# A fused attention and expert kernel: the first item's first 256 rows turned by VectorE, cast by GpSimd

## The chip, the core and the metric

The kernel runs on one core of a Trainium2 chip. The metric is the device time of one execution in microseconds, the median of several runs; lower is better.

## The reference

Two stages. The first is an attention with random features; its output, as rows of 512, goes into a mixture of experts with a capacity.

```python
# 4 batches, 8 heads, 576 positions, 64 columns; omega is 128 x 64
def phi(x):                       # x already scaled by 64 ** -0.25
    h = x @ omega.T - sum(x * x) / 2
    return exp(h - max(h)) / sqrt(128)
kv  = phi(k).T @ v                # per batch and head: 128 x 64
z   = sum(phi(k), over positions)
out = (phi(q) @ kv) / (phi(q) @ z + 1e-6)

# x: 2304 rows of 512, out of the heads; 8 experts, w1 512 x 1024, w2 1024 x 512, capacity 576
logits = x @ w_gate;  e = argmax(logits);  p = softmax(logits)[e]
# each expert takes its rows in order, up to the capacity
y   = relu(x @ w1[e]) @ w2[e]
out = p * y for the rows kept, 0 for the others
```

## The kernel before

Only TensorE can multiply matrices; it writes PSUM, eight banks of 2 KB a partition. Everything is f32, and the expert products are made from split operands: a rounded part (`hi`) and the rest (`lo`), so that one product is three matmuls (hi by hi, lo weights by hi, hi weights by lo).

**Keys.** A first loop (steps below 0) projects the keys, takes their maxima and exponentials and sums `kv` for each batch and head. The gate's weights are multiplied into `kv` as extra columns, so that the routing scores come out of the same numerators as the attention.

**Queries.** Then come 18 query tiles of 128 rows, one a step. The code's step `t` runs from 0 to 20, and the work on one tile is spread over four steps:

- In step t TensorE projects tile t (`project`, output pjq, two banks) from a chunk of queries (`qraw`, three tiles a chunk; `load_q(c + 2)` is issued in the last step of chunk c). ScalarE copies one half to `d`, VectorE takes the maxima of both halves (L192), GpSimd adds the maxima to one half of `d` (L837), ScalarE adds those of the other half (L852).
- In step t + 2 TensorE transposes `d` (L782, output qtr, two banks) and ScalarE takes the exponentials (L843, qpT).
- In step t + 3 TensorE multiplies by `kv` (`numer`, L654, output qacc) and VectorE normalises (`normalise`: denominators L678, reciprocal L679, product `xr` L682, scores L685). SP stores the rows to `x_d` in DRAM. The rows that are stored in step s are thus those of tile s - 3. The numerators of steps 3 to 17 and 19 share one PSUM tile (`pair`, one buffer), those of steps 18 and 20 have banks of their own.

All engines run their instructions in program order. Smaller jobs are generators that the loop resumes at fixed places (`run`): a job that yields "E" goes on at the end of a step, one that yields "P" behind the GpSimd addition, at most `most` such pieces in a step.

**The first item.** The rows are given out to experts later, but the first item's expert is known as soon as row 0 is scored, since the kernel's first item is batch 0 with the expert of its first row (rows of it that go to another expert get a scale of 0, and rows that no such item holds go through a branch at the end). `first_item` reads that expert and loads its four `w1` chunks (`load_w`, 512 KB each) at steps given by `W1_LOADS`. `first_splits` splits each chunk on GpSimd in five pieces: one `hi` of 128x1024 (L135) and four `lo` of 128x256 (L140), 20 pieces in all. Before the change it begins with the load of the second chunk, so that its pieces come from step 9 on.

The item needs its rows transposed (features on the partitions), as `xhi` and `xlo`, 576 columns. Its columns are made in two ways before the change:

- Rows 0 to 255 (two tiles): in steps 3 and 4 GpSimd copies `xr` into a scratch tile `xt` (L690); in steps 6 to 9 (`FIRST_AT`) TensorE transposes 64 rows a step, four instructions of 64x64 among those of `d` (L782, output xtri), and `copy_x` makes `xhi` on ScalarE (L430) and `xlo` on VectorE (L432).
- Rows 256 to 575: `first_rows` loads them from `x_d` behind step 15 with SP (`load_x`, four DMAs, 32 partitions each, L401). In steps 18 and 19 VectorE turns them in 32x32 blocks (`turn_x`, L406, 640 columns each time, into `xt`), ScalarE makes `xhi` (L411) and GpSimd `xlo` (L412).

Behind the numerators of step 20 TensorE starts the first item's products (`mm1`, L705 to L707), first those with columns 0 to 255 of `xhi` and `xlo`. The other items follow, each with its rows loaded and turned by the second way.

Of the kernel before, what the change touches and what calls it, by code (L numbers as in the profile page):

```python
# [22 lines left out]
NT = N // 128  # L23
# [13 lines left out]
AHEAD = [(0, 0)]  # L37
NJ = 11
FIRST_LOAD = 15
W1_LOADS = (0, 6, 9, 12)  # L40
W2_LOADS = 16
FIRST_AT = (6, 7, 8, 9)
BRANCH_AT = 4
EPS = 1e-6 * M
BIG = 1048576.0
# [18 lines left out]
def attention_moe(ctx, tc, kT, qT, va, om, wg, w1, w2, cap, ident, tri, desc, lst, tab0, out):  # L64
# [83 lines left out]
    def start(gen):  # L148
        tasks.append([gen, None])
# [245 lines left out]
                in_offset=bass.IndirectOffsetOnAxis(ap=big["idx"][0:n, i, 2:3], axis=0),  # L395
            )

    def load_x(rows, b0=0):
        src = x_d[rows, :].rearrange("(b r) (q c) -> q r b c", r=32, q=4)
        for q in range(4):  # L400
            nc.sync.dma_start(big["xz"][32 * q : 32 * q + 32, b0:, :], src[q])  # L401


    def turn_x(b0, b1, o=0, eng=nc.vector):
        t = big["xt"][:, o : o + b1 - b0, :].rearrange("p b (k r) -> p b k r", k=4)
        nc.vector.transpose(t, big["xz"][:, b0:b1, :].rearrange("p b (a k) -> p b k a", k=4))  # L406
        t = t.rearrange("p b k r -> p k b r")
        hi, lo = (big[x][:, :, 32 * b0 : 32 * b1].rearrange("p k (b r) -> p k b r", r=32) for x in ("xhi", "xlo"))

        def split():  # L410
            nc.scalar.copy(hi, t)  # L411
            eng.tensor_tensor(lo, t, hi.bitcast(F32), op=ALU.subtract)  # L412

        return split

    def transpose_x(i, nm, at):
        n = sub_n[i]
# [186 lines left out]
    def first_item():  # L604
        yield from pause(6)
        e0 = const.tile([1, E + 2], F32, name="e0")
        e0i = const.tile([1, 1], I32, name="e0i")
        lg0 = lg[0:1, 0, :]
        nc.vector.tensor_reduce(e0[:, E : E + 1], lg0, op=ALU.max, axis=AX.X)
        yield  # L610
        nc.vector.scalar_tensor_tensor(
            e0[:, 0:E], lg0, e0[:, E : E + 1], desc_sb[0:1, :], op0=ALU.is_ge, op1=ALU.mult
        )
        yield
        nc.vector.tensor_reduce(e0[:, E + 1 : E + 2], e0[:, 0:E], op=ALU.max, axis=AX.X)
        yield
        nc.vector.tensor_scalar(e0i, e0[:, E + 1 : E + 2], -1.0, float(E), op0=ALU.mult, op1=ALU.add)
        yield
        ev = nc.sync.value_load(e0i[0:1, 0:1], min_val=0, max_val=E - 1)
        for c in range(4):  # L620
            while step[0] < W1_LOADS[c]:
                yield "E"
            load_w(1, c, ev)
            if c == 1:
                start(first_splits())
            yield "E"
        while step[0] < W2_LOADS:
            yield "E"
        for c in range(4):
            load_w(2, c, ev)  # L630
            yield "E"
# [9 lines left out]
                split_w_lo(1, c, nc.gpsimd, k)  # L641

    xr_l = {}

    def first_rows():
        load_x(slice(32 * NBA, SLOTS), NBA)
# [15 lines left out]
    def normalise(t, acc, whole):  # L664
# [19 lines left out]
            )  # L684
        nc.vector.tensor_reduce(lg[:, t, :], xr[:, D + 1 : ROW, :], op=ALU.add, axis=AX.X)  # L685
        nc.sync.dma_start(x_d[t * 128 : (t + 1) * 128, :], xr[:, 0:D, :].rearrange("p c h -> p (c h)"))
        if t < 2:

            xr_l[t] = big["xt"][:, 4 * t : 4 * t + 4, :]
            nc.gpsimd.tensor_copy(xr_l[t], xr[:, 0:D, :].rearrange("p c h -> p (c h)").rearrange("p (m k) -> p k m", k=4))  # L690

    HALVES = [(0, 256), (256, SLOTS)]

# [42 lines left out]
    for n in range(NK + NT + 3):  # L736
# [24 lines left out]
        if 0 <= t - 2 < NT:  # L761
            d = d_l.pop(t - 2)
            trs = [bank((3 + i, (2, SM)[i])[t > NT], f"qtr{n}{i}") for i in range(2)]

            parts = [
                [(trs[i][:, u * 64 : (u + 1) * 64], d[64 * i : 64 * i + 64, u, :], i) for u in range(H)] for i in range(2)
            ]

            if t in FIRST_AT:
                k0 = FIRST_AT.index(t)  # L770
                i = k0 % 2
                tr = bank(SM, f"xtri0{k0}")
                rows = slice(64 * i, 64 * i + 64)
                x0 = xr_l[k0 // 2]
                parts[i][0:0] = [
                    (tr[:, k * 64 : (k + 1) * 64], x0[rows, k, :], i) for k in range(4)
                ]
                start(copy_x(tr, 64 * k0, 64))
            for x in chain(*zip_longest(*parts)):
                if x is not None:  # L780
                    rows = slice(64 * x[2], 64 * x[2] + 64)
                    nc.tensor.transpose(x[0], x[1], id_sb[rows, rows])  # L782
# [47 lines left out]
        else:  # L830
            if t < NT:
# [4 lines left out]
                maxima(mx, 0, d[:, 0:4, :])  # L836
                nc.gpsimd.tensor_tensor(d[:, 0:4, :], d[:, 0:4, :], spread(mx, 0), op=ALU.add)  # L837
                d_l[t] = d
            run("P", times=2, most=2)
            if 0 <= t - 2 < NT:  # L840
                qpT = qp.tile([128, 2, H * 64], F32, tag="qpT", name=f"qpT{t}", bufs=2)
                for i in range(2):
# [15 lines left out]
            if 0 <= t - 3 < NT:  # L858
                normalise(t - 3, acc_l[0], whole)
                if t == 3:  # L860
                    start(first_item())
            if t in (NT, NT + 1):

                b0 = NBA + 5 * (t - NT)
                split_x = turn_x(b0, b0 + 5, b0 - NBA, nc.gpsimd)
# [8 lines left out]
        if n < NK:  # L874

            for k in range(KB, 2 * B):
                if (9 * (k - KB) + 8) // KG + 2 == n:
                    load_k(k // 2, k % 2)
            if n == 3:
                start(setup())  # L880
            if n in (NK - 4, NK - 2):
                load_q(0 if n == NK - 4 else 1)
        if t == FIRST_LOAD:
            first_rows()
    qstack.close()
# [317 lines left out]
```

## Time and profile before

| | us |
|---|---|
| median of 3 runs | 261.82 (260.41 to 262.20) |
| the profiled execution | 260.95 |
| its span, first to last instruction | 259.2 |
| TensorE busy, matmuls | 253.7 |
| TensorE busy, weight loads (beside the matmuls) | 232.7 |
| VectorE busy | 167.2 |
| ScalarE busy | 148.8 |
| GpSimd busy | 42.6 |

The key loop ends and the query steps begin at about 46 us; step 6 begins at 62.0, step 10 at 74.3, step 17 at 93.6, and the first item's products at 101.5. TensorE's granted clock is the full 2.4 GHz in all slices. A row of the profile gives the start of an instruction or of a run of equal ones, how long it took, its engine, its line and what it writes and reads; PE is TensorE, DVE VectorE, ACT ScalarE, POOL GpSimd, and SPq the queue of SyncE, which issues most of the DMAs.

### The profile page before, as it was taken

To read this page: it belongs to the slowest core of one execution; us is meant where nothing else is said; L and a number is where in the kernel's file an instruction comes from. 1 tells how busy PE (TensorE), PEld (TensorE's weight loads), DVE (VectorE), ACT (ScalarE), POOL (GpSimd) and SP (SyncE) were. 2 spreads that over 40 slices of the span, in tenths; PEclk is the share of its full clock that TensorE was granted. 3 is DMA by queue.
4 is the path that set the end of the run, shared out by engine and by line. 5 is a ranking of instruction groups with operands and counts; after the bars stand their busy time and mean duration, and the time that the engine had idled before them with its cause. 6 is when DMAs were issued, how large, how long until landed. Compare 5 with 4: busy or idle time off the path is not lost. (4 is left out here: it accounts for less than half of the span.)

```text
span 259.2 us, 7581 instructions
## 1 busy us (share of the span) xinstructions
PE 253.7 (98%) x3058; PEld 232.7 (90%) x3058; DVE 167.2 (65%) x351; ACT 148.8 (57%) x374; POOL 42.6 (16%) x61
## 2 busy tenths in 40 slices
PE   7999999999999999999999999999999999999994
PEld 6999999999999999999988789999888999998882
DVE  3999888779999998655763745566850064667500
ACT  3788888899999995326402536552361155524611
POOL 1002000255369896200000000000000000000000
PEclk9999999999999999999999999999999999999999
DMA  7999870034976769990059619992012897950121
GB/s 204 390 382 349 285 254 3 5 122 149 311 234 207 275 169 289 373 390 21 1 134 276 206 49 311 213 286 66 3 40 66 293 245 206 326 164 0 49 93 48
DMA packets 35171, 48.54 MB, mean 187 GB/s; under 512 B 2290, under 2 KB 23410, under 8 KB 35122
## 3 DMA queue, kind: packets, MB, share of 16 engines
q1 hardware_dynamic: 34002, 46.39, 57.0%
q10 hardware_dynamic: 1120, 1.52, 1.9%
q8 instruction: 28, 0.46, 0.7%
q14 instruction: 21, 0.17, 0.2%
HBM read 35.97 MB, written 11.93 MB: 185 GB/s over the span
## 5 line engine op out<-in xcount | busy, mean ns | idle before, releaser
L705 PE MATMUL hi<-xhi,w1hi 128*128 128x256 f32 (+1 forms) x192 | 56.7, 295 | 0.0
L706 PE MATMUL hi<-xhi,w1lo 128*128 128x256 f32 (+1 forms) x192 | 56.4, 294 | 0.0
L707 PE MATMUL hi<-xlo,w1hi 128*128 128x256 f32 (+1 forms) x192 | 56.3, 293 | 0.0
L718 DVE SCALAR_TENSOR_TENSOR hlo<-hi,hhi 128x256 fp32r<-128x256 f32 x48 | 20.2, 420 | 44.4 <-ACT hhi L716 22.4
L716 ACT ACTIVATE hhi<-hi 128x256 fp32r<-128x256 f32 x48 | 18.3, 384 | 36.1 <-PE hi L707 36.1
L898 PE MATMUL yi<-w2hi,hhi 128*128 128x512 f32 x96 | 37.5, 390 | 0.3 <-issue 0.3
L899 PE MATMUL yi<-w2hi,hlo 128*128 128x512 f32 x96 | 37.4, 389 | 0.0
L705 PEld LDWEIGHTS hi<-xhi,w1hi 128*128 128x128 f32 x192 | 36.0, 188 | 0.3
L706 PEld LDWEIGHTS hi<-xhi,w1lo 128*128 128x128 f32 x192 | 36.0, 188 | 0.1
L707 PEld LDWEIGHTS hi<-xlo,w1hi 128*128 128x128 f32 x192 | 36.0, 187 | 0.0
L192 DVE TENSOR_REDUCE mx<-pjk 128x4 f32<-128x512 f32 (+1 forms) x38 | 23.4, 656 | 4.2 <-PE pjk L175 4.0
L837 POOL TENSOR_TENSOR d<-d,mx 128x512 f32<-128x512 f32 x18 | 18.7, 1039 | 42.2 <-DVE mx L192 39.8
L175 PE MATMUL pjk<-om_s,kraw 64*128 64x128 f32 x288 | 23.9, 300 | 0.2
L818 ACT ACTIVATE ex<-pjk,mx 128x128 f32<-128x128 f32 x72 | 20.6, 368 | 6.0 <-DVE mx L192 5.7
L904 PE MATMUL yi<-w2lo,hhi 128*128 128x512 f32 x96 | 23.7, 389 | 0.0
L654 PE MATMUL qacc<-kv_sb,qpT 128*64 128x73 f32 x576 | 22.5, 230 | 0.1
L898 PEld LDWEIGHTS yi<-w2hi,hhi 128*128 128x128 f32 x96 | 18.0, 188 | 4.3 <-issue 0.7
L175 PEld LDWEIGHTS pjk<-om_s,kraw 64*128 64x128 f32 x288 | 20.4, 203 | 1.5 <-DMA kraw<-kT 0.6
L175 PE MATMUL pjq<-om_s,qraw 64*128 64x128 f32 x288 | 21.6, 284 | 0.0
L904 PEld LDWEIGHTS yi<-w2lo,hhi 128*128 128x128 f32 x96 | 18.0, 188 | 3.7
L899 PEld LDWEIGHTS yi<-w2hi,hlo 128*128 128x128 f32 x96 | 18.0, 188 | 3.6
L852 ACT ACTIVATE d<-pjq,mx 128x128 f32<-128x128 f32 x72 | 21.0, 404 | 0.3 <-DVE mx L192 0.3
(148 smaller groups left out, 416.4 us busy)
## 6 DMA issues: line engine op xcount, KB each, us to landing
w1raw<-w SPq DMA_DIRECT2D x16, 512.0 KB, 6.8
w2raw<-w SPq DMA_DIRECT2D x16, 512.0 KB, 5.8
qraw<-qT SPq DMA_DIRECT2D x6, 768.0 KB, 6.3
x_d<-xr SPq DMA_DIRECT2D x18, 256.0 KB, 4.3
v<-va SPq DMA_DIRECT2D x7, 650.0 KB, 6.5
xg<-x_d SPq DMA_DIRECT2D x12, 288.0 KB, 7.6
kraw<-kT SPq DMA_DIRECT2D x5, 576.0 KB, 7.0
out<-ysi SPq DMA_DIRECT2D x9, 256.0 KB, 2.1
```

The lines of the kernel that those rows point to most:

```text
L175: nc.tensor.matmul(banks[i][:, k * M : (k + 1) * M], parts[k][rows, :], om_s[rows, :], start=True, stop=True)
L192: nc.vector.tensor_reduce(mx[:, a : a + src.shape[1]], src, op=ALU.max, axis=AX.X, negate=True)
L654: nc.tensor.matmul(acc[i][r : r + 64, p * ROW : (p + 1) * ROW], qpT[:, r // 64, (4 * i + p) * 64 : (4 * i + p) * 64 + 64], kv_sb[(t * 128 ...
L705: nc.tensor.matmul(pt, whi_[:, k, fs], xhi[:, k, sl], start=(k == 0), stop=False)
L706: nc.tensor.matmul(pt, wlo_[:, k, fs], xhi[:, k, sl], start=False, stop=False)
L707: nc.tensor.matmul(pt, whi_[:, k, fs], xlo[:, k, sl], start=False, stop=(k == 3))
L718: nc.vector.scalar_tensor_tensor(lo, src, 0.0, hi.bitcast(F32), op0=ALU.max, op1=ALU.subtract)
L818: nc.scalar.activation(ex[:, o + k, :], q[0][:, k * M : (k + 1) * M], AF.Exp, bias=mx[:, o + k : o + k + 1], scale=1.0)
L852: nc.scalar.activation(d[:, 4 + k, :], pj[1][:, k * M : (k + 1) * M], AF.Identity, bias=mx[:, 4 + k : 5 + k], scale=1.0)
L898: nc.tensor.matmul(pt, hhi[:, f, sl], w2_at(w_hi, f), start=(f == 0), stop=False)
L899: nc.tensor.matmul(pt, hlo[:, f, sl], w2_at(w_hi, f), start=False, stop=False)
L904: nc.tensor.matmul(pt, hhi[:, f, sl], w2_at(w_lo, f), start=False, stop=(f == 7))
```

## The change

The second way is used for rows 0 to 255 as well, in smaller portions, and the first way goes. Behind steps 6 and 7 SP loads these rows from `x_d`, two of the four DMAs each time (128 KB each, behind what the step's end issues). In steps 11 to 16 VectorE turns one block of 32 rows (128 columns of the tile) a step, in step 17 two, each behind the step's normalisation. In steps 12, 14, 16 and 17 GpSimd makes `xhi` and `xlo` of two blocks (`split_early`, 256 columns each). GpSimd's copies of steps 3 and 4, TensorE's 16 transposes, and the casts and subtractions of `copy_x` in steps 6 to 9 are no longer there.

The splits of `w1` start with the load of the first chunk instead of the second (their pieces then come from step 6 on), and the number of pieces a step is 2 up to step 10, 2 in steps 11, 13 and 15, 1 in steps 12 and 14, none in steps 16 and 17, and 2 again from step 18 on.

```diff
--- before.py
+++ after.py
@@ -37,9 +37,9 @@
 AHEAD = [(0, 0)]
 NJ = 11
 FIRST_LOAD = 15
+EARLY = {11 + i: (i, i + 1 + (i == 6)) for i in range(7)}
 W1_LOADS = (0, 6, 9, 12)
 W2_LOADS = 16
-FIRST_AT = (6, 7, 8, 9)
 BRANCH_AT = 4
 EPS = 1e-6 * M
 BIG = 1048576.0
@@ -395,10 +395,10 @@
                 in_offset=bass.IndirectOffsetOnAxis(ap=big["idx"][0:n, i, 2:3], axis=0),
             )
 
-    def load_x(rows, b0=0):
+    def load_x(rows, b0=0, b1=NB, qs=range(4)):
         src = x_d[rows, :].rearrange("(b r) (q c) -> q r b c", r=32, q=4)
-        for q in range(4):
-            nc.sync.dma_start(big["xz"][32 * q : 32 * q + 32, b0:, :], src[q])
+        for q in qs:
+            nc.sync.dma_start(big["xz"][32 * q : 32 * q + 32, b0:b1, :], src[q])
 
 
     def turn_x(b0, b1, o=0, eng=nc.vector):
@@ -412,6 +412,13 @@
             eng.tensor_tensor(lo, t, hi.bitcast(F32), op=ALU.subtract)
 
         return split
+
+    def split_early(t):
+        b0, b1 = EARLY[t - (t < max(EARLY))][0], EARLY[t][1]
+        x = big["xt"][:, b0:b1, :].rearrange("p b (k r) -> p k b r", k=4)
+        hi, lo = (big[n][:, :, 32 * b0 : 32 * b1].rearrange("p k (b r) -> p k b r", r=32) for n in ("xhi", "xlo"))
+        split_hi(hi, x, nc.gpsimd)
+        split_lo(lo, x, hi, nc.gpsimd)
 
     def transpose_x(i, nm, at):
         n = sub_n[i]
@@ -621,7 +628,7 @@
             while step[0] < W1_LOADS[c]:
                 yield "E"
             load_w(1, c, ev)
-            if c == 1:
+            if c == 0:
                 start(first_splits())
             yield "E"
         while step[0] < W2_LOADS:
@@ -641,8 +648,6 @@
                 split_w_lo(1, c, nc.gpsimd, k)
 
 
-
-    xr_l = {}
 
     def first_rows():
         load_x(slice(32 * NBA, SLOTS), NBA)
@@ -684,10 +689,6 @@
             )
         nc.vector.tensor_reduce(lg[:, t, :], xr[:, D + 1 : ROW, :], op=ALU.add, axis=AX.X)
         nc.sync.dma_start(x_d[t * 128 : (t + 1) * 128, :], xr[:, 0:D, :].rearrange("p c h -> p (c h)"))
-        if t < 2:
-
-            xr_l[t] = big["xt"][:, 4 * t : 4 * t + 4, :]
-            nc.gpsimd.tensor_copy(xr_l[t], xr[:, 0:D, :].rearrange("p c h -> p (c h)").rearrange("p (m k) -> p k m", k=4))
 
     HALVES = [(0, 256), (256, SLOTS)]
 
@@ -766,16 +767,6 @@
                 [(trs[i][:, u * 64 : (u + 1) * 64], d[64 * i : 64 * i + 64, u, :], i) for u in range(H)] for i in range(2)
             ]
 
-            if t in FIRST_AT:
-                k0 = FIRST_AT.index(t)
-                i = k0 % 2
-                tr = bank(SM, f"xtri0{k0}")
-                rows = slice(64 * i, 64 * i + 64)
-                x0 = xr_l[k0 // 2]
-                parts[i][0:0] = [
-                    (tr[:, k * 64 : (k + 1) * 64], x0[rows, k, :], i) for k in range(4)
-                ]
-                start(copy_x(tr, 64 * k0, 64))
             for x in chain(*zip_longest(*parts)):
                 if x is not None:
                     rows = slice(64 * x[2], 64 * x[2] + 64)
@@ -836,7 +827,7 @@
                 maxima(mx, 0, d[:, 0:4, :])
                 nc.gpsimd.tensor_tensor(d[:, 0:4, :], d[:, 0:4, :], spread(mx, 0), op=ALU.add)
                 d_l[t] = d
-            run("P", times=2, most=2)
+            run("P", times=2, most=(2 if t % 2 else 1) if 11 <= t < 16 else 2 * (t < 16 or t >= NT))
             if 0 <= t - 2 < NT:
                 qpT = qp.tile([128, 2, H * 64], F32, tag="qpT", name=f"qpT{t}", bufs=2)
                 for i in range(2):
@@ -859,6 +850,10 @@
                 normalise(t - 3, acc_l[0], whole)
                 if t == 3:
                     start(first_item())
+            if t in EARLY:
+                turn_x(*EARLY[t], EARLY[t][0])
+                if t % 2 == 0 or t == max(EARLY):
+                    split_early(t)
             if t in (NT, NT + 1):
 
                 b0 = NBA + 5 * (t - NT)
@@ -880,6 +875,8 @@
                 start(setup())
             if n in (NK - 4, NK - 2):
                 load_q(0 if n == NK - 4 else 1)
+        if t in (6, 7):
+            load_x(slice(0, 32 * NBA), 0, NBA, range(2 * t - 12, 2 * t - 10))
         if t == FIRST_LOAD:
             first_rows()
     qstack.close()
```

## Rows read from the trace of the kernel before

**Rows 1.** The page, first part: busy time, share and instructions of each engine

```profile
PE 253.7 (98%) x3058; PEld 232.7 (90%) x3058; DVE 167.2 (65%) x351; ACT 148.8 (57%) x374; POOL 42.6 (16%) x61
```

**Rows 2.** Table by stage: stretch, its length, busy time by engine, clock, DMA share, GB/s

```profile
77.06:79.83 2.77, 2.77 (x69) 2.62 (x65) 2.56 (x7) 2.61 (x9) 2.42 (x3) 1.00 0.84 281
```

**Rows 3.** Timeline of TensorE: start us, us, engine, line, operation, names, shapes, count

```profile
70.08 1.25 PE L654 MATMUL qacc<-kv_sb,qpT 128*64 128x73 f32 x32
71.32 1.16 PE L175 MATMUL pjq<-om_s,qraw 64*128 64x128 f32 x16
72.29 0.22 PE L782 MATMUL xtri<-id_sb,xt 64*128 64x64 f32 x1
...
73.12 1.25 PE L654 MATMUL qacc<-kv_sb,qpT 128*64 128x73 f32 x32
...
75.30 0.66 PE L782 MATMUL qtr<-id_sb,d 64*128 64x64 f32 x16
75.88 1.25 PE L654 MATMUL qacc<-kv_sb,qpT 128*64 128x73 f32 x32
77.06 1.16 PE L175 MATMUL pjq<-om_s,qraw 64*128 64x128 f32 x16
...
78.65 1.25 PE L654 MATMUL qacc<-kv_sb,qpT 128*64 128x73 f32 x32
...
96.39 0.89 PE L782 MATMUL qtr<-id_sb,d 64*128 64x64 f32 x16
...
101.51 0.39 PE L705 MATMUL hi<-xhi,w1hi 128*128 128x256 f32 x1
```

**Rows 4.** Timeline of SP's queue: the issue of the query chunk for step 9

```profile
63.81 0.57 SPq L209 DMA_DIRECT2D qraw<-qT  x1
```

**Rows 5.** DMA issues of 63.7 to 64.5 and of 67.2 to 68.0: last column us to landing

```profile
qraw<-qT SPq DMA_DIRECT2D x1, 768.0 KB, 7.4
...
w1raw<-w SPq DMA_DIRECT2D x1, 512.0 KB, 6.2
```

**Rows 6.** Transposes of VectorE, grouped by line and shape: busy us, mean ns

```profile
L406 DVE STREAM_TRANSPOSE xt<-xg 128x1280 f32<-128x1280 f32 x3 | 7.3, 2440 | 0.0
L406 DVE STREAM_TRANSPOSE xt<-xg 128x1024 f32<-128x1024 f32 x3 | 5.9, 1980 | 5.7 <-DMA xg<-x_d 5.7
...
L406 DVE STREAM_TRANSPOSE xt<-xg 128x640 f32<-128x640 f32 x2 | 2.8, 1388 | 0.0
```

**Rows 7.** Timeline of VectorE, steps 8 to 11

```profile
70.44 0.68 DVE L192 TENSOR_REDUCE mx<-d 128x4 f32<-128x512 f32 x1
71.03 0.41 DVE L432 TENSOR_TENSOR xlo<-xtri,xhi 128x256 fp32r<-128x256 f32 x1
...
77.18 0.17 DVE L678 TENSOR_SCALAR den<-qacc 128x8 f32<-128x8 f32 x1
...
77.62 0.77 DVE L682 TENSOR_TENSOR xr<-qacc,rec 128x584 f32<-128x584 f32 x1
...
79.15 0.68 DVE L192 TENSOR_REDUCE mx<-d 128x4 f32<-128x512 f32 x1
```

**Rows 8.** Timeline of ScalarE, step 17

```profile
95.43 1.09 ACT L843 ACTIVATE qpT<-qtr 128x512 f32<-128x512 f32 x2
```

**Rows 9.** Groups of GpSimd by line and shape: busy us, mean ns

```profile
L837 POOL TENSOR_TENSOR d<-d,mx 128x512 f32<-128x512 f32 x18 | 18.7, 1039 | 42.2 <-DVE mx L192 39.8 <-DVE den L678 1.6 <-DVE e L615 0.7
...
L140 POOL TENSOR_TENSOR w1lo<-w1raw,w1hi 128x256 fp32r<-128x256 f32 x16 | 11.4, 729 | 0.2
...
L135 POOL TENSOR_SCALAR w1hi<-w1raw 128x1024 fp32r<-128x1024 f32 x4 | 4.2, 1050 | 0.0
```

**Rows 10.** DMA issues of 73.0 to 73.6: last column us to landing

```profile
qraw<-qT SPq DMA_DIRECT2D x1, 768.0 KB, 5.3
```

**Rows 11.** Table by stage: before the second query chunk, and the row loads

```profile
70.90:73.30 2.40, 2.40 (x55) 2.22 (x52) 2.30 (x7) 2.23 (x8) 1.04 (x1) 1.00 0.41 144
...
93.80:97.40 3.60, 3.60 (x85) 3.34 (x87) 3.32 (x9) 3.44 (x12) 3.57 (x4) 1.00 1.01 211
```

## The prediction

> **What bounds the kernel now.** The page's first part comes first: TensorE is busy for 98% of the span [rows 1], so only what takes work or waits out of TensorE's own queue can move the end. The change lies in the query loop (steps 6 to 17, 62 to 96 us). The table by stage shows what to look for there: a plain step, such as step 11, lasts 2.77 us, all of it with TensorE busy, while VectorE works 2.56 us, ScalarE 2.61 and GpSimd 2.42 [rows 2]. TensorE sets the pace, but VectorE has only some 0.2 us to spare.
>
> TensorE's timeline tells why. In step 9, one of the four with transposes of x, the transposes run from 72.29 to the numerators at 73.12, 0.83 us; in step 10, without x, from 75.30 to 75.88, 0.58 us [rows 3]. Behind 101.51, where the first matmuls of the expert work start, TensorE goes on without a gap to speak of up to the last output, so a step that becomes shorter is worth its time only if the start at 101.51 comes earlier.
>
> **The change part by part, removed work.** Sixteen transposes in four steps: 4 x 0.25 = 1.00 us of TensorE. With them go four ScalarE casts and four VectorE subtractions; those engines follow TensorE in these steps, and their leaving is worth nothing beside it. So are the two GpSimd copies of steps 3 and 4.
>
> Only part of the 1.00 us arrives. The query projection of step 9 reads a query chunk whose load is issued at 63.81 [rows 4] and takes 7.4 us [rows 5]: it lands at 71.2. The projection starts at 71.32; the numerators before it start at 70.08 and take 1.18 us from start to next start (75.88 to 77.06), so without a wait it would start at 71.26 [rows 3]. The load now lands just in time, and costs 0.06 us. With steps 6, 7 and 8 shorter by 0.25 each, TensorE arrives at 71.26 - 0.75 = 70.51, and the load is issued no earlier (it stands behind a store of step 5, which the change doesn't touch). TensorE then waits some 0.8 us, and the 0.75 is gone. Step 9's own 0.25 us is all that stays. If the load lands by 70.4, the gain is 1.00 + 0.06 = 1.06.
>
> **The new transposes on VectorE.** One block (128 columns) in each of steps 11 to 16, two in step 17, each behind the step's normalisation and ahead of the next step's maxima. No row has one of 128 columns. Those shown take 1.39 us for 640, 1.98 for 1024 and 2.44 for 1280 [rows 6]. From both sides: a fifth of the 640 is 0.28 us, with no fixed part; the line through 640 and 1280 (0.21 us per 128, fixed part 0.34) gives 0.55. Back to back on VectorE the next instruction starts some 0.09 us before the last one ends: the maxima take 0.68, and the next starts 0.59 later (70.44 to 71.03) [rows 7]. So the queue pays 0.19 to 0.46; I take 0.33, in the middle, since the line through 1024 and 1280 alone (0.23 per 128, fixed 0.14, so 0.28 in the queue) is nearer to the low end and the one through 640 to the high one.
>
> VectorE's queue without waits: from the denominators (77.18) to the second maxima (79.15) 1.97 us, and 0.59 for those, 2.56 [rows 7]. With 0.33 more: 2.89, over TensorE's 2.765 by 0.125. From step 11 on VectorE would set the pace. What releases TensorE is the product that reads the numerators' bank (xr): the next numerators overwrite that bank. It ends at 77.62 + 0.77 = 78.39 and the next numerators start at 78.65 [rows 3, 7]; with 0.09 for the signal the slack is 0.17 us. The last numerators in that one bank are those of step 17, released by the product of step 16; five transposes (steps 11 to 15) stand before it. Step 18 uses other banks, and what VectorE does behind step 17 (its transpose of two blocks, 0.5 to 0.7 us) has no maxima behind it: it is covered by TensorE's steps 18 and 19. Delay at step 17's numerators: 5 x 0.125 - 0.17 = 0.455 us.
>
> Some of that comes back. Step 18's transposes take 0.89 us instead of step 10's 0.66 [rows 3], since they wait for banks that ScalarE still reads: its two exponentials start at 95.43 and take 1.09, to 96.52 [rows 8]. A TensorE that comes later finds them free: 0.23 back. Loss: 0.455 - 0.23 = 0.225 us. At the ends of the price: 0.19 makes 2.75 a step, no loss; 0.46 makes 5 x 0.255 - 0.40 = 0.875.
>
> The Trainium skill ("VectorE: DVE Perf Modes", section "The three transpose paths") gives 311 ns for a 128x128 transpose of bf16 on VectorE. By that the queue would pay some 0.22, an estimate from that page, and the loss would be 5 x 0.015, under the slack: none. No row here has that size or that type, and the page gives no fixed part for f32.
>
> **GpSimd.** The weight pieces begin three steps earlier (step 6 instead of 9), two a step up to step 10: ten of twenty are done by then. Step 11: hi and lo; 12: one lo; 13: two lo; 14: one hi; 15: two lo; 16, 17: none; 18: two. A hi piece takes 1.05, a lo piece 0.73, the addition on d 1.04 [rows 9]. Each pair of casts is 256 columns twice: the subtraction 0.73 by the lo piece; the hi between a quarter of 1.05 and the whole, I take 0.35. Four pairs, 4.3 us. Per step 11 to 17: 2.8, 2.8, 2.5, 3.2, 2.5, 2.1, 2.1, sum 18.0 against 7 x 2.77 = 19.4: it fits, at a cost of nothing. What hides it is that d is read two steps later; a step in which GpSimd runs 0.4 us over is made good in the next. At the hi's upper end the sum is 20.8, and the last pair comes 1.4 us later. Without that it is ready at about 99.5: step 17's product ends at 78.39 + 7 x 2.765 = 97.7, then 0.7 for the small reduction and the two blocks and 1.08 for the casts. It is due at 101.51, so it stays hidden at either price.
>
> Waits that this adds on GpSimd: hi pieces now stand close to their loads' landing, by at most 0.5 us; behind them queues d, with two steps of slack. The last transposes (18, 19) write blocks that GpSimd's casts read; those casts are over by then.
>
> **The new loads.** Four DMAs of 128 KB, two behind steps 6 and 7, on SP behind a store and a weight load: issued about 67.9 to 70.6, so behind the query chunk that lands at 71.2. A weight load that is issued in between (67.2 to 68.0, 6.2 us to landing) lands at some 73.5, behind the chunk [rows 5]: transfers there land in the order of issue, so I count nothing against the chunk. Behind them is the chunk for step 12: issued at 73.0, landing 5.3 us later, 78.3 [rows 10]; it is needed at 79.83 - 0.25 = 79.6. The engines are 41% busy in the 2.4 us before that issue [rows 11], room for 1.4 us of the 2.5 that 512 KB take at the 211 GB/s of the row loads [rows 11]. The rest, 1.1 us, is less than the 1.3 of slack: no cost. Without that room: 2.5 - 1.3 = 1.2 us late.
>
> **Sum.** Removed 0.25, added 0.225: -0.03 us on the profiled execution's 260.95 (span 259.2 and 1.75 around it), which is 0.87 under the median of the three runs. Carried to the median 261.82: 261.8.
>
> **The rivals.**
> - The load for step 9 doesn't hold TensorE (it lands by 70.4). For it: the chunk for step 12, as large, takes 5.3 us [rows 10], so the 7.4 may be chance. Against it: nothing in its issue changes, nor in what stands ahead of it. -1.06 + 0.225 = -0.84: 261.0.
> - The transpose is dearer, and VectorE is the bound of steps 11 to 16. Place: the bank of the numerators, from step 13 on. It decides from a queue price of about 0.40 (5 x 0.195 - 0.40 = 0.575, more than twice the 0.25 that is gained). At 0.46: -0.25 + 0.875 = +0.62: 262.4. For it: 0.2 us of room in every step; against it: only five transposes count.
> - The new loads push the chunk for step 12 behind its need: -0.25 + 0.2 + 1.2 = +1.2: 263.0. Against it: the room just named.
> - The change doesn't bring the early start of the expert work, because the last casts of step 17 come after 101.5; they would have to be 2.0 us later than worked out. I give it no chance of its own.
>
> **How the numbers follow.** Forecast 0.50, early landing 0.25, dear transpose 0.17, late chunk 0.08. The forecast alone covers 261.6 to 262.1. The three runs lie between 260.41 and 262.20, so the range takes 0.9 below the early landing and 0.5 above the dear transpose: 260.1 to 262.9. One per cent, 2.6 us, is about what a measurement of this kernel tells from no change; no case reaches it. For what I have not seen, 0.04 on each side; within 1%: 0.92.
>
> **What would show it.** In the changed profile: transposes 0.58 us in steps 6 to 9 (removal right); a gap on TensorE before the projection of step 9, some 0.8 us, ended by the query load (if it is missing, the early landing); the 128-column transpose's mean, 0.28 to 0.55, and steps 12 to 17 at 2.77 or at 2.89 with VectorE free of gaps; the first expert matmul at about 101.5; GpSimd's last pair of casts before it. A gap before step 12's projection, or steps of 3 us and more, would make the prediction wrong.

## The result and the profile after

The changed kernel takes 262.17 us (median of 22 runs, 260.82 to 264.77), the kernel before, run beside it, 260.85 (259.68 to 262.20): ratio 1.0051, 95% interval 1.0031 to 1.0071. It is slower by 1.3 us, inside the one per cent, but not the change of nothing that was forecast. The profiled execution took 262.26 us, its span 260.4.

The page of the changed kernel, first part: TensorE has 16 instructions less [rows 1], is busy 0.1 us less, and has a longer span around that.

```profile
PE 253.6 (97%) x3042; PEld 232.8 (89%) x3042; DVE 168.1 (65%) x354; ACT 147.6 (57%) x370; POOL 44.7 (17%) x67
```

TensorE's timeline of the changed kernel, steps 9 and 10 and the start of the expert work. The brackets are idle time and what ended it.

```profile
68.43 1.16 PE L175 MATMUL pjq<-om_s,qraw 64*128 64x128 f32 x16
...
70.02 1.25 PE L659 MATMUL qacc<-kv_sb,qpT 128*64 128x73 f32 x32
71.57 1.16 PE L175 MATMUL pjq<-om_s,qraw 64*128 64x128 f32 x16 [0.31 <-DMA qraw<-qT]
...
74.33 0.82 PE L175 MATMUL pjq<-om_s,qraw 64*128 64x128 f32 x9
76.07 0.60 PE L175 MATMUL pjq<-om_s,qraw 64*128 64x128 f32 x6 [0.92 <-issue]
...
98.19 0.79 PE L773 MATMUL qtr<-id_sb,d 64*128 64x64 f32 x16
...
103.27 0.38 PE L706 MATMUL hi<-xhi,w1hi 128*128 128x256 f32 x1
```

The transposes of x are gone, and the expert work starts at 103.27 instead of 101.51 [rows 3]. Two gaps are new. Ahead of step 9's projection there is a short one (0.31 us, where 0.8 was forecast). In the middle of step 10's projection TensorE stops for 0.92 us with every operand there: the wait is put down to "issue", that is to nothing that the profile shows.

The table by stage of the changed kernel, steps 9, 10 and 14 (columns as in [rows 2]):

```profile
71.57:74.33 2.76, 2.76 (x64) 2.61 (x65) 2.48 (x5) 2.25 (x8) 1.61 (x3) 1.00 1.00 283
74.33:78.39 4.06, 3.14 (x68) 2.91 (x65) 2.73 (x6) 2.62 (x9) 3.36 (x5) 1.00 1.03 332
...
86.74:89.61 2.87, 2.84 (x67) 2.65 (x65) 2.77 (x8) 2.64 (x9) 2.87 (x4) 1.00 1.06 379
```

Step 10 lasts 4.06 us with all DMA engines busy. Step 14 lasts 2.87, 0.1 more than a plain step before [rows 2]; there VectorE is the bound: its timeline has no gap over 0.15 us from step 12 to step 17.

The two DMA windows that hold TensorE's own instruction packet, the stretch of the kernel before first (its 70 to 72 us), then the changed kernel's 72 to 74. The second line's queue brings instructions, a packet of 16 KB, and the share is of all 16 engines.

```profile
q1 hardware_dynamic: 449, 0.56, 77.7%
q8 instruction: 1, 0.02, 3.0%
```

```profile
q1 hardware_dynamic: 781, 0.56, 101.8%
q8 instruction: 1, 0.02, 3.3%
...
qraw<-qT SPq DMA_DIRECT2D x1, 768.0 KB, 7.2
```

The packet starts 24.2 us behind the first query projection before the change (22.8 in a second execution), 26.9 after. The last line is the query chunk for step 12, issued at 73.00: 7.2 us to landing instead of 5.3 [rows 10].

To compare executions, the next table sets each one's time from its first query projection (at 46.04 us in the profile before, 46.78 after) to the projections of steps 9, 12 and 17 and to the first expert matmul, each a difference of two starts in TensorE's timeline. The key stage ahead of it scatters by 2 us (41.9 to 44.0 from its first projection, in these runs) without any edit there, so spans are not compared.

| kernel, executions | step 9 | step 12 | step 17 | expert |
|---|---|---|---|---|
| before, 2 | 25.28, 25.21 | 33.79, 33.74 | 47.60, 47.55 | 55.47, 55.53 |
| changed, 3 | 24.79, 24.53, 24.82 | 34.37, 34.36, 33.80 | 48.55, 49.02, 47.98 | 56.49, 57.01, 56.06 |
| changed, no new loads, 2 | 24.43, 24.67 | 32.73, 32.95 | 46.80, 47.03 | 54.91, 56.00 |
| before + loads, 2 | 25.21, 25.21 | 33.74, 33.98 | 47.55, 47.79 | 55.42, 55.66 |
| before + loads in whole rows | 25.21 | 34.32 | 48.14 | 56.12 |
| before + loads twice | 25.21 | 36.91 | 52.25 | 60.12 |
| before - transposes, 2 | 24.65, 24.82 | 33.18, 33.19 | 46.99, 47.00 | 54.94, 55.01 |
| changed, one load a step | 24.94 | 33.22 | 48.35 | 56.58 |
| changed, blocks in every other step, 2 | 24.53, 25.14 | 33.83, 33.57 | 47.65, 47.38 | 55.97, 55.44 |
| changed, blocks in steps 13 to 17, loads behind 9 and 10 | 25.16 | 33.45 | 48.41 | 56.56 |
| the same, query chunks asked for earlier | 25.50 | 33.78 | 47.82 | 55.79 |
| changed, loads behind steps 11 and 12, 2 | 24.73, 24.85 | 33.02, 33.14 | 50.60, 51.25 | 58.87, 60.35 |

### The profile page after: what moved, and what is told of

It reads as the page before. It is cut to its first block, busy times and chain, and to the rows that moved or that the text cites. A ratio compares the mean times of both kernels' runs of the same rounds, so it can differ in the third digit from the quotient of the medians.

```text
span 260.4 us, 7559 instructions
## 1 busy us (share of the span) xinstructions
PE 253.6 (97%) x3042; PEld 232.8 (89%) x3042; DVE 168.1 (65%) x354; ACT 147.6 (57%) x370; POOL 44.7 (17%) x67
## 5 line engine op out<-in xcount | busy, mean ns | idle before, releaser
L175 PE MATMUL pjk<-om_s,kraw 64*128 64x128 f32 x288 | 24.5, 308 | 0.2 <-DMA kraw<-kT 0.2
L406 DVE STREAM_TRANSPOSE xt<-xg 128x128 f32<-128x128 f32 (+4 forms) x15 | 19.2, 1277 | 6.6 <-DMA xg<-x_d 6.6
L175 PEld LDWEIGHTS pjk<-om_s,kraw 64*128 64x128 f32 x288 | 21.0, 210 | 1.3 <-DMA kraw<-kT 0.5
L659 PEld LDWEIGHTS qacc<-kv_sb,qpT 128*64 128x64 f32 x576 | 20.1, 136 | 1.6
```

The lines of the kernel that those rows point to most:

```text
L175: nc.tensor.matmul(banks[i][:, k * M : (k + 1) * M], parts[k][rows, :], om_s[rows, :], start=True, stop=True)
L659: nc.tensor.matmul(acc[i][r : r + 64, p * ROW : (p + 1) * ROW], qpT[:, r // 64, (4 * i + p) * 64 : (4 * i + p) * 64 + 64], kv_sb[(t * 128 ...
```

## The experiments

Two theories. **DMA:** the new loads take time from the DMA engines that other transfers need: TensorE's instructions and the query chunks. **VectorE:** its transposes make it the bound of steps 11 to 16, and that is the loss. The expectations also call the first one the fetch theory and the second one the pace or transposes theory. Two more stand in them: chance (the one profile had bad luck) and layout (the stop comes from where the instruction blocks of the shorter program end, not from the loads). The code below shows the main lines of each edit; `...` marks lines left out between two places.

**The changed kernel, twice more** (no edit).

> The changed kernel once more, to see whether TensorE's stall of step 10 (0.9 us in the middle of a projection, put down to issue, with the instruction packet between 72 and 74 us instead of 70 to 72) is there every time. Fetch theory (the new loads fill the DMA engines when TensorE's next instruction block is due): the stall comes again, 0.5 to 1.3 us within steps 9 to 12, ratio 1.003 to 1.007. Chance theory (the one profile had bad luck, the loss is VectorE's pace): no gap over 0.3 us put down to issue, steps 13 to 17 at 2.86 us, ratio 1.001 to 1.003.

> The changed kernel a third time, as the partner of the other three on the same chip. DMA theory: TensorE's gap put down to issue in step 10 again (0.3 to 1.3 us), instruction packet later than 25 us behind the first projection; ratio 1.002 to 1.007.

Ratios 1.0032 (1.0009 to 1.0055) and 1.0046 (1.0017 to 1.0076). Both show the stop in step 10, and its size changes. TensorE's waits (total, times, longest), the first execution's and then the second's:

```profile
PE pjq L175 <- issue: 1.2, 1, 1.2
...
PE pjq L175 <- DMA qraw<-qT: 0.6, 1, 0.6
```

```profile
PE pjq L175 <- issue: 0.3, 1, 0.3
```

The instruction packet starts 26.9 and 26.0 us behind the first projection, and TensorE goes on at 29.3 and 28.7. The first also waits for the query chunk of step 15. The loss is real, and the stop comes in all three executions; the holds for query chunks differ from one to the next.

**The kernel before once more** (no edit).

> The kernel before against itself: every theory expects a ratio of 1.000 within 0.002. Its profile shows how far the start (the wait for the first keys) and the waits of the query loop scatter without any change: all theories expect no gap put down to issue in the query loop.

1.0016 (0.9991 to 1.0040): a difference below 0.25% is not resolved here.

**The loads alone, and the changed kernel without them.** To the kernel before:

```diff
+        if t in (6, 7):
+            load_x(slice(0, 32 * NBA), 0, NBA, range(2 * t - 12, 2 * t - 10))
```

> The kernel before with nothing but the four new loads of the first 256 rows added behind steps 6 and 7; nobody reads what they bring. Fetch theory: TensorE stalls for issue, 0.5 to 1.3 us, in steps 9 to 12, and the kernel is 0.5 to 1.5 us slower (ratio 1.002 to 1.006). Layout theory (the stall comes from where the shorter program's instruction blocks end, not from the loads): TensorE's program is unchanged, no stall, ratio 0.999 to 1.001. Transposes theory (VectorE's pace is the loss): ratio 0.999 to 1.001.

> The kernel before with the four new loads alone, a second time, for a second profile and twice the runs. DMA theory: ratio 1.002 to 1.006, and in this profile a gap on TensorE in steps 8 to 13 (the first one had none). Chance theory: ratio 0.999 to 1.002.

From the changed kernel the same two lines are taken out, and the seven transposes (of eight blocks) read a tile of zeros:

```diff
-                turn_x(*EARLY[t], EARLY[t][0])
+                b0, b1 = EARLY[t]
+                turn_x(b0, b1, b0, raw=zero_sb[:, 0 : 128 * (b1 - b0)].rearrange("p (b c) -> p b c", c=128))
```

> The changed kernel without the four new loads; the early transposes read a tile of zeros instead, so the first 256 columns of the first item are not the reference's. TensorE's program is that of the changed kernel, instruction for instruction. DMA theory (the new loads make TensorE's next instruction block and the query chunks late, and this is the larger part of the loss): no gap put down to issue in step 10, the instruction packet back at 23 to 25 us behind the first query projection, only VectorE's pace of 2.86 us in steps 13 to 17 stays; ratio to before 0.998 to 1.001. Pace theory (VectorE's 0.46 us and the hold of step 9 are the loss, the stall is chance): the same as the changed kernel, 1.003 to 1.005. Layout theory: the stall of 1 us stays, 1.003 to 1.005.

> The changed kernel without the four new loads, transposes reading zeros, a second time (the first 256 columns of the first item are not the reference's). DMA theory: no gap put down to issue, instruction packet at 23.5 to 25 us behind the first projection, 0.7 to 1.3 us less than the changed kernel. Chance theory: a gap as in the changed kernel, less than 0.3 us of difference.

Loads alone: 1.0043 (1.0016 to 1.0070) and 1.0035 (1.0009 to 1.0062). All the rest without them: 1.0007 (0.9985 to 1.0029) and 0.9994 (0.9967 to 1.0022). So by these ratios the loads carry the loss, whichever kernel they stand in. In the kernel before, though, neither execution with them shows the stop that was expected, and the expert work starts 0.1 us earlier and 0.2 later: how they cost there is not shown. In the changed kernel it is. Without them step 10 of the changed kernel has no stop and the usual length, as the table by stage of the first of these executions shows:

```profile
73.08:75.84 2.76, 2.76 (x68) 2.61 (x64) 2.54 (x7) 2.60 (x8) 2.68 (x4) 1.00 0.91 264
```

TensorE's instruction list is the same there as in the changed kernel; its packet starts 24.5 and 24.3 us behind the first projection. The second execution has a stop of its own for "issue", 0.9 us, just ahead of the expert work, which makes its 56.00.

The trace can be asked whether these stops are waits for instructions. Twelve executions here have the changed kernel's TensorE list. Six of them stop for "issue" in the query loop, seven times in all, and always at one of three places of the list: the second is 256 recorded TensorE instructions (weight loads, matmuls and synchronisation) behind the first, the third 1280, five times 256, behind the second. A packet comes every two steps or so, which hold about as many (128 weight loads and 128 matmuls). Each time TensorE goes on 1.2 to 1.5 us behind the end of a packet. At the other places that lie a multiple of 256 away it passes without such a stop wherever the packet had ended 1.6 us or more ahead. So the layout theory is right about where a stop can fall; whether one comes depends on when the packet lands.

**Which property of the loads.** The kernel before with the same 512 KB as two DMAs of whole rows of 2 KB, and with each load made twice:

```diff
+        if t in (6, 7):
+            a = t - 6
+            nc.sync.dma_start(big["xg"][:, a, :], x_d[128 * a : 128 * a + 128, :])
```

```diff
+        if t in (6, 7):
+            for b0 in (0, NBA):
+                load_x(slice(0, 32 * NBA), b0, b0 + NBA, range(2 * t - 12, 2 * t - 10))
```

> The kernel before with the same 512 KB loaded as two DMAs of 128 whole rows (2 KB pieces) instead of four of 512-byte pieces, read by nobody. If bytes decide: the same cost as the loads alone, ratio 1.002 to 1.006. If the number of pieces decides: a quarter of it, ratio 0.999 to 1.002.

> The kernel before with the four new loads made twice (eight DMAs, 1 MB, behind steps 6 and 7), read by nobody. DMA theory (from 62 to 80 us the DMA engines have no room left, and what comes later is TensorE's instruction block or a query chunk): about 2.5 us more of all DMA engines than with the loads once, so gaps on TensorE of 1.5 to 3 us between steps 8 and 13, ratio 1.006 to 1.012. Chance theory (the loads are covered; the 0.4% of the loads alone was scatter): ratio 0.999 to 1.002, no gap over 0.3 us.

Whole rows: 1.0039 (1.0011 to 1.0067), as dear as the short pieces; so it is not the pieces' size. Twice the bytes: 1.0137 (1.0091 to 1.0183), three to four times the loss. TensorE's waits show it ahead of step 12:

```profile
PE pjq L175 <- DMA qraw<-qT: 3.1, 1, 3.1
```

The chunk for step 12 lands 32.3 us behind the first projection in the kernel before, 33.4 to 34.2 with the loads, 36.8 with twice as many. The first 512 KB eat most of the slack. The second are not the engines' time alone: the chunk is also asked for 2.9 us later (29.9 instead of 27.0 behind the first projection), since the extra loads stand ahead of it in SP's queue and one of them is held there, and its flight is 6.8 us instead of 5.3. In SP's waits and timeline:

```profile
SPq L401 <- DMA w1raw<-w: 1.9, 1, 1.9
```

```profile
75.84 1.13 SPq L209 DMA_DIRECT2D qraw<-qT  x1
```

**The transposes of TensorE alone.** The kernel before, with its casts reading the copy that was not transposed:

```diff
-                parts[i][0:0] = [
-                    (tr[:, k * 64 : (k + 1) * 64], x0[rows, k, :], i) for k in range(4)
-                ]
-                start(copy_x(tr, 64 * k0, 64))
+                start(copy_x(None, 64 * k0, 64, x0[:, :, 64 * i : 64 * i + 64]))
```

> The kernel before without TensorE's 16 transposes of x; the casts and subtractions of steps 6 to 9 read the untransposed copy, so the first 256 columns of the first item are not the reference's. It prices the removal alone. If the query load of step 9 holds TensorE as forecast: a gap of 0.3 to 0.8 us before the projection of step 9, gain 0.25 to 0.7 us (ratio 0.997 to 0.999). If it doesn't: gain 1.0 us (ratio 0.996). Layout theory: a stall put down to issue of some 0.9 us in step 10 and no gain. Fetch theory: no such stall.

> The kernel before without TensorE's 16 transposes of x, a second time (the first 256 columns of the first item are again not the reference's). If the removal is worth what its first profile showed in the query loop (0.5 us): ratio 0.997 to 0.999 in this set and the two sets together below 1.000. If the wait for the query chunks gives all of it back: 0.999 to 1.001, with the projection of step 12 no earlier behind the first one than 33.2 us.

1.0018 (0.9997 to 1.0039) and 0.9994 (0.9969 to 1.0019); in the timeline the expert work starts 0.5 us earlier (54.94 and 55.01 against 55.50). The gain is there and is too small for the comparison of medians; the first ratio missed what was expected, and neither execution has the gap of 0.3 us or more that was expected ahead of step 9. It is not the price of the whole removal either: the four subtractions of `copy_x` stay here, and with them VectorE has no gap in steps 9 and 10 and sets their length: 2.89 and 2.88 us in the first execution, where a plain step takes 2.76. In its timeline, from step 9 to step 10:

```profile
71.68 0.68 DVE L192 TENSOR_REDUCE mx<-pjq 128x4 f32<-128x512 f32 x1
72.28 0.67 DVE L192 TENSOR_REDUCE mx<-d 128x4 f32<-128x512 f32 x1
72.87 0.41 DVE L433 TENSOR_TENSOR xlo<-xt,xhi 128x256 fp32r<-128x256 f32 x1
73.21 0.16 DVE L679 TENSOR_SCALAR den<-qacc 128x8 f32<-128x8 f32 x1
```

**Other places for the loads and for VectorE's blocks.** First, one load behind each of steps 6 to 9; second, VectorE's blocks in steps 11, 13, 15 and 16 and four blocks in step 17; third, blocks in 13, 15, 16 (two) and 17 (four) and the loads behind steps 9 and 10; fourth, that and each query chunk asked for right behind the projection. GpSimd's casts and weight pieces are placed to match.

```diff
+        if t in (6, 7, 8, 9):
+            load_x(slice(0, 32 * NBA), 0, NBA, (t - 6,))
```

```diff
+EARLY = {11: (0, 1), 13: (1, 2), 15: (2, 3), 16: (3, 4), 17: (4, 8)}
```

```diff
+EARLY = {13: (0, 1), 15: (1, 2), 16: (2, 4), 17: (4, 8)}
...
+        if t in (9, 10):
+            load_x(slice(0, 32 * NBA), 0, NBA, range(2 * t - 18, 2 * t - 16))
```

```diff
+            if t - QB[c] == 2 and c + 2 < len(QB) - 1:
+                load_q(c + 2)
```

> The changed kernel with the four loads spread: one behind each of steps 6, 7, 8 and 9 instead of two behind 6 and 7. Fetch theory: the DMA engines are less full between 69 and 73 us, the stall of step 10 shrinks below 0.5 us or goes, 0.4 to 1.0 us faster than the changed kernel (ratio to before 0.999 to 1.003). Layout theory and chance theory: same as the changed kernel (ratio 1.003 to 1.007 and 1.001 to 1.003).

> The changed kernel with its loads as they are, but VectorE's transposes in steps 11, 13, 15 and 16 (one block) and 17 (four blocks), casts in steps 13, 16 and 17 to match. A transpose in every other step costs nothing, since VectorE makes up 0.2 us in the step between. Pace theory: steps 12 to 17 at 2.77 us, 0.3 to 0.6 us faster than the changed kernel, ratio to before 0.999 to 1.002. DMA theory: steps 12 to 17 at 2.77 us as well, but the stall of 1.0 to 1.3 us in step 10 stays, ratio 1.001 to 1.004.

> The changed kernel with transposes in every other step, a second time, now beside the changed kernel itself on the same chip. Pace theory: 0.4 to 0.6 us less than the changed kernel (0.0015 to 0.0025 of the ratio). DMA theory with the pace as the second part: the same difference, and a gap put down to issue or to a query chunk of 0.3 to 1.3 us in steps 9 to 12.

> Two moves at once: the loads behind steps 9 and 10 instead of 6 and 7, and the transposes in steps 13 and 15 (one block), 16 (two) and 17 (four). DMA theory: no stall in steps 9 to 11 (the DMA engines are no fuller there than before the change), gain of the removed transposes less a hold of 0.1 to 0.5 us in step 9: 0.4 to 0.9 us faster than before, ratio 0.9965 to 0.9985; a late query chunk for step 15 (up to 0.5 us) would eat part of it. Pace theory: 0.3 to 0.6 us faster than the changed kernel, ratio 0.999 to 1.002. Layout theory: the stall of 1 us is in step 10 still.

> The same with the query chunks' loads issued right behind the projection that frees their buffer, in place of behind the step's store (about 1.5 to 2 us earlier on SP). The hold theory of the forecast (step 9 waits for its query chunk): the chunk lands before 70.5, no gap ahead of the projection of step 9, another 0.1 to 0.5 us: ratio to before 0.995 to 0.998. If the chunk lands no earlier (the DMA engines decide, not the issue), the same as without it.

First: 1.0053 (1.0024 to 1.0082). Step 10 is whole, but the last rows land late: VectorE's first transpose waits for them, and TensorE for the product behind it. In VectorE's and in TensorE's timeline:

```profile
82.16 0.43 DVE L406 STREAM_TRANSPOSE xt<-xg 128x128 f32<-128x128 f32 x1 [0.92 <-DMA xg<-x_d]
```

```profile
85.02 1.25 PE L659 MATMUL qacc<-kv_sb,qpT 128*64 128x73 f32 x32 [0.93 <-DVE xr L687]
```

Second: 0.9986 (0.9955 to 1.0016) and 1.0025 (1.0000 to 1.0050). Steps 12 to 17 last 13.82 and 13.81 us, as before the change (13.81), instead of 14.18: the blocks' cost is gone when they stand in every other step. Third: 1.0012 (0.9987 to 1.0037); step 10 is whole and the chunk for step 15 lands late (42.7 us behind the first projection), with a gap of 1.1 us ahead of its projection (the profile names ScalarE's `d` there, but the projection starts 0.14 us behind the chunk's last piece). Fourth: 1.0017 (0.9995 to 1.0039); step 9 no longer waits, but TensorE stops for "issue" in step 8's projection (0.8 us), its packet 2 us late. The first is slower than the kernel before, the others are not told from it. The first, the third and the fourth came out above the ratios that the DMA theory expected, the second's first set below.

**The loads behind the last query chunk** (blocks in steps 15 to 17), twice:

```diff
+EARLY = {15: (0, 1), 16: (1, 4), 17: (4, 8)}
...
+        if t in (11, 12):
+            load_x(slice(0, 32 * NBA), 0, NBA, range(2 * t - 22, 2 * t - 20))
```

> The changed kernel with the transposes of tiles in steps 15 to 17 only (one, three and four blocks) and the four new loads behind steps 11 and 12, where the query chunk for step 18 has been asked for already. If the loads cost by what is queued behind them on the DMA engines, no query chunk and no instruction block is behind them any more: step 10 and the projections of steps 12 and 15 show no hold, step 12's projection starts 32.7 to 33.2 us behind the first one, the first expert matmul 54.9 to 55.3 us behind it, and the ratio to the kernel before is 0.9975 to 0.9995. If instead the first weight pieces or the last casts become late by the loads' new place, the expert stage starts with a wait and the ratio is 1.000 to 1.002. If the transposes on VectorE are what costs, step 17 is late by 0.4 us or more and the ratio is above 1.001 with no hold on a DMA.

> The same kernel once more, for a second look and a second ratio: 0.9975 to 0.9995 if the loads' place was the cost, 1.000 to 1.002 if a late cast or weight piece takes its place.

The first half of the DMA theory's forecast held: no stop in step 10, step 12 at 33.02 and 33.14 us, no wait for the chunks of steps 12 and 15. Yet this is the slowest place of all: 1.0137 (1.0091 to 1.0183) and 1.0139 (1.0096 to 1.0182). GpSimd's timeline of the first shows the new victim, the last weight chunk, and TensorE's what stands behind it:

```profile
85.76 0.73 POOL L142 TENSOR_TENSOR w1lo<-w1raw,w1hi 128x256 fp32r<-128x256 f32 x1
91.04 1.04 POOL L137 TENSOR_SCALAR w1hi<-w1raw 128x1024 fp32r<-128x1024 f32 x1 [4.55 <-DMA w1raw<-w]
92.05 1.04 POOL L830 TENSOR_TENSOR d<-d,mx 128x512 f32<-128x512 f32 x1
```

```profile
88.56 1.25 PE L661 MATMUL qacc<-kv_sb,qpT 128*64 128x73 f32 x32
89.74 1.16 PE L177 MATMUL pjq<-om_s,qraw 64*128 64x128 f32 x16
93.14 1.12 PE L775 MATMUL qtr<-id_sb,d 64*128 64x64 f32 x16 [2.25 <-POOL d L830]
...
96.28 1.16 PE L177 MATMUL pjq<-om_s,qraw 64*128 64x128 f32 x16
```

The chunk's load (issued at 83.38) lands 7.6 us later, where the kernel before needs 5.1 and 5.3. The cast stands at the head of GpSimd's queue, the addition on `d` behind it, and step 16's transposes need that `d`. The step takes 6.54 us instead of 2.76. Less those 3.78, the expert work would start at 55.1, in the forecast 54.9 to 55.3. In the second execution the same wait is 2.71 us, the step takes 7.06, and TensorE is slow into step 17 as well (1.28 us more up to its numerators); less both, 54.8. The place was right for the query chunks and wrong for the weights.

## Why the prediction was wrong

The forecast was a change of -0.03 us; the table gives +1.02 (means 56.52 and 55.50), the medians +1.32. That the measured time lies in the range is luck: the three runs it started from have a median 0.97 us above that of the 22, so the forecast of no change stood that much too high. Of the cases, the rival of the late chunk (+1.2 us, 263.0, given 0.08) was nearest in mechanism and in size of the change.

- **Step that failed: "the new loads", put at no cost.** Between the changed kernel with and without them, step 12 comes 1.34 us later (34.18 against 32.84): in the mean step 10 is 1.18 us longer by the stop, and step 9 starts 0.16 later. The backlog had been worked out well: 1.1 us, and the chunk for step 12 lands 33.4 to 33.8 instead of 32.3 behind the first projection. Two things were missed. The slack of 1.3 held only if the removed work were lost at step 9; TensorE, without the loads, comes to step 12 at 32.84, so 0.5 was left. And only named data transfers were counted: the packet with TensorE's own instructions was not looked for, and it is the dearer of the two. In the four executions with this stop (three of the changed kernel, one with blocks in every other step, where it is 0.19 us) the packet starts 25.4 to 26.9 us behind the first projection; where it starts at 22.8 to 24.8, there is none in that step.
- **Removed work, forecast 0.25: mis-sized.** Without the loads step 12 comes 0.93 us earlier (32.84 against 33.77), nearly the whole 1.00. Wherever the chunk for step 9 is asked for at the old place, it lands 24.3 to 25.2 us behind the first projection, 25.1 and 25.2 in the two executions of the kernel before. It was read there as "just in time" from one execution; after the removal the hold is 0.3 us at most in the changed kernel, not 0.8. Why it lands sooner there isn't settled. That the casts and subtractions leave "is worth nothing" holds only with the transposes there: with the transposes gone and the subtractions kept, step 12 comes 0.58 us earlier, not 0.93.
- **VectorE's transposes, 0.455 us at step 17's numerators: right.** Steps 12 to 17 last 14.18 us in two of the three executions (the third has the hold at step 15) and 14.07 without the loads, against 13.81: 0.37. The numerators of step 17 start 1.68 us behind their projection (95.33 to 97.01) instead of 1.58: 0.47 in all. One block takes 0.42 us; the next instruction starts 0.33 behind it, the value that was taken. In VectorE's timeline of the changed kernel, step 13's numerators to step 14's:

```profile
85.59 0.42 DVE L406 STREAM_TRANSPOSE xt<-xg 128x128 f32<-128x128 f32 x1
85.92 0.67 DVE L192 TENSOR_REDUCE mx<-pjq 128x4 f32<-128x512 f32 x1
...
88.46 0.42 DVE L406 STREAM_TRANSPOSE xt<-xg 128x128 f32<-128x128 f32 x1
```

  From block to block 2.87 us, forecast 2.89, and TensorE's steps follow (2.87). The Trainium skill ("VectorE: DVE Perf Modes", section "The three transpose paths") gives 311 ns for bf16. This f32 block took 0.42; by that figure of the Trainium skill the loss would, as an estimate, have been none.
- **The 0.23 us given back in step 18: hardly any.** Its transposes take 0.79 us instead of 0.89 [rows 3], but the way from step 17's projection to the expert work, with the 0.10 just named in it, is 0.08 longer (means 8.00 and 7.92).
- **GpSimd's casts, hidden: right here, by a cover that can go.** In its timeline the last pair is

```profile
100.62 0.40 POOL L135 TENSOR_SCALAR xhi<-xt 128x256 fp32r<-128x256 f32 x1 [0.88 <-DVE den L683]
101.11 0.73 POOL L140 TENSOR_TENSOR xlo<-xt,xhi 128x256 fp32r<-128x256 f32 x1
```

  ready at 101.84, needed at 103.27. The hi cast takes 0.40 (0.35 taken). That a weight load holds GpSimd's queue "by at most 0.5 us" was wrong: in the changed kernel it was 1.15, 1.44 and 1.78 us around the end of step 9, and up to 0.9 without the new loads. TensorE never waited for it there; with the loads moved it was 4.55, and TensorE did.

The terms together, from the means of the table: up to step 12 -0.93 + 1.34 = +0.41; from there to step 17 +0.53 (0.37 of pace, 0.16 the third part of one hold of 0.5); behind it +0.08: +1.02.

**What stays open.** In two executions the loads alone delay the expert work by 0.0 and 0.2 us, in whole rows by 0.6, while the ratios put their loss at 0.9 us and more. In both, the part from the first expert matmul to the end lasts 157.9 us against 157.7 and 157.4 in the kernel before, but the changed kernel has 157.1 to 157.9 there; in one the key stage, ahead of the loads, is 1.1 us longer. That isn't enough to say where the rest goes. That the stop for "issue" is the late packet is read from places and times that agree in every execution; no run moved the packet alone. With the new loads in the same place the packet was late in four executions of five (25.4 to 26.9, once 23.9), and what decides that is not shown. No version tried is shown to beat the kernel before.

## What to carry to other kernels

Where the DMA engines are nearly full, as here from 64 to 80 us in the changed kernel (a share of 0.86 to 1.05 in each 2 us), a load that nobody waits for is not free: add its bytes to the backlog and its place to the queue that issues it, and look for everything due behind it, the instruction packets of the bounding engine among it. Work out each slack against the changed schedule, not against the old one, and take a landing time from more than one execution. Moving such a load only changes the victim; test the place by the queue that stands behind the transfer that it delays.

## What the runs showed of the hardware

- TensorE's instructions come through the same DMA engines, 16 KB a packet, and by the places of the stops one packet for 256 recorded instructions. In the changed kernel one started 1.5 to 2.7 us later than in the same kernel without the new loads, and TensorE stopped for 0.3 to 1.2 us in the middle of a projection with its operands there; it went on 1.2 to 1.5 us behind the packet's end.
- A long gap can cost more than its length. In the last experiment TensorE waited 2.25 us; the table by stage then shows a granted clock of 0.74 for the step, and full speed in the next:

```profile
89.74:96.28 6.54, 4.29 (x67) 3.90 (x64) 2.93 (x8) 3.66 (x12) 5.24 (x7) 0.74 0.77 200
96.28:99.05 2.77, 2.77 (x68) 2.62 (x65) 2.54 (x6) 1.64 (x4) 1.84 (x4) 1.00 0.24 78
```

  The transposes behind the gap took 1.12 us instead of 0.66 and the numerators 2.16 instead of 1.25, as at 1.2 GHz instead of 2.4: some 1.4 us on top of the wait. In the second execution, behind 2.71 us, the slow rows go on for about 6 us, into step 17. After the 0.92 us in step 10 of the changed kernel, and the 1.18 of its second execution, the clock stayed at 1.00. The kernel with the loads twice has the same behind its 3.1 us, a granted clock of 0.70 in step 12: step 17 is late by 4.7.
